# The last 128 output columns: skip product added in the seed of the PSUM bank, plain-copy evacuation, and a store cut into two halves of rows

## The chip, the cores and the metric

The kernel runs on one core of one Trainium2 chip. The metric is the device time of one execution in microseconds (us). The kernel before takes 177.33 us, the median of three runs (177.13, 177.33 and 177.41).

The engines of the core are named as in the profile: PE is TensorE (matrix products), PEld its weight loads, DVE is VectorE, ACT is ScalarE, POOL is GpSimd and SP is SyncE, which does nothing here but issue DMAs. ACT issues a few DMAs too. The engines run their own instruction queues strictly in order and wait for each other through counting semaphores.

## The reference

Two blocks read the same layer-normed rows and their results are added to the input. Block A is a diagonal state-space model, block B a gated feed-forward. The input x has 2048 rows of D = 512 columns, the state P = 512, the hidden width F = 1376; inputs and output are bfloat16.

```python
def _A_ref(x, ...):                      # x is the normed input
    Lam_bar = exp(dt * Lam)
    Bu = einsum("bld,pd->blp", x, B_bar)
    for t in range(L): h = Lam_bar * h + Bu[:, t]; hs.append(h)
    return 2.0 * einsum("blp,dp->bld", hseq, Cmat).real + x * Dskip
def _B_ref(x, w_gate, w_up, w_down):
    return (gelu(x @ w_gate) * (x @ w_up)) @ w_down
xn = layernorm(x)
return x + _A_ref(xn, ...) + _B_ref(xn, ...)
```

So every output element is a sum of four things: x itself, the skip product xn * Dskip, the product of the states with C, and the product of the hidden activations with w_down.

## The kernel before

**Tiling.** The 2048 rows are four blocks of 512 rows; a block is four row tiles of 128 rows (tile number tt = 4 * block + j). Per block the program does: layer norm (LN, LN_act), a transpose of the normed rows by DMA (TR), the two feed-forward products (GU), the input product of the state model (BU), the recurrence on DVE (CHAIN: rotations by cosine and sine tables around a scan), and last the output product (DN). DN(b) adds, for each row tile j, eleven matmuls over the hidden activations (`hidden`) and eight over the states (`states`) into one PSUM bank of 128 x 512 fp32.

**Who adds what in DN.** `seed` (L873 to L876) writes x into the PSUM bank with an ACT copy before the first matmul of the tile; all matmuls accumulate on top of it. XD holds the skip product xn * Dskip (made on DVE, L671). `store` (L897 to L905) evacuates the bank: DVE adds XD to it and writes bfloat16 into one of four OUTB buffers (L902), and a DMA stores the 128 rows (L904).

**The last row tile.** DN(3, tail=384) cuts the fourth tile of the last block into columns 0 to 383 (its own bank) and columns 384 to 511 (an extra bank, `xbank`). Each part has its seed, 19 matmuls, evacuation and store; the store of the 384 columns is issued from ACT, every other one from SP. The 128-column part is the last work of the program.

**The start.** Block 0 is the only one whose feed-forward is computed in part with the rows as stationary operand, from centred but not yet scaled rows: `GT_k` and `GT_mm` (L696 to L714) fill a bank with gate columns beside up columns, for row tile j and column part u (u = 0, 1, 2 are 256 columns wide, u = 3 is 128). `GT_evac` (L716 to L726) empties it: ACT takes the gelu of the gate half (L721), DVE multiplies by the up half and writes H0[j] (L724, called "H0 product" below). The scale 1/sqrt(var) of the layer norm goes in there as a per-row scalar. Eight banks are in use, so the later parts reuse banks of the earlier ones:

```python
for (j, u), bank in zip([(3, 0), (3, 1), (0, 2), (0, 3), (1, 2), (1, 3), (2, 2), (2, 3), (3, 2), (3, 3)],
                        (6, 7, 0, 1, 2, 3, 4, 5, 0, 7)):
    GT_mm(j, u, bank)
    GT_evac(j, u, bank)
```

Part (3, 2) is thus computed into bank 0, which part (0, 2) had six parts earlier; the matmuls of (3, 2) need the gelu and the H0 product of (0, 2) to be done. The six parts before this loop use banks 0 to 5, as acc(j, u) = 2 * j + u for j < 3, u < 2.

**The parameters of the state model.** Three rows of 512 parameters are loaded and transposed by a DMA on the SP queue (`tr_par`, L515, behind the weight loads of `load_W`). `params` (L556 to L565) starts from them: POOL computes exp(log_dt) with one power instruction (L557), DVE multiplies it with Lambda_im (L558, called "theta product" below) and goes on with a few tiny instructions (L559 to L565).

**What sets the order of each queue.** The program is recorded first and then ordered by a planner in the kernel itself (class Sched). Every recorded operation has a duration written out by hand and its dependencies from the buffers it reads and writes. PE and SP keep the order in which they were recorded. DVE, ACT and POOL do not: a list scheduler chooses for them, in time order, the ready operation with the earliest due time. The due times come from a backward pass from the end of the plan; forward and backward passes alternate six times (`schedule`, L136 to L148) and the order with the shortest planned span is taken. `emit` (L286 to L337) then writes the queues, with waits on the counting semaphores where an operation needs another engine's result. A DMA counts in the plan as 2000 ns plus one ns per 350 bytes, behind the DMAs planned before it. The backward pass starts from the last operations of the program, so durations and dependencies there take part in every due time.

**The end.** `emit` also makes SP wait for the stores: before its second-to-last DMA for all stores but the last five, before its last DMA for the next three, and after it for the last two.

Of the kernel before, what the change touches and what calls it, by code (L numbers as in the profile page):

```python
# [9 lines left out]
ALU = mybir.AluOpType  # L10
ACTF = mybir.ActivationFunctionType
# [66 lines left out]
class Sched:  # L78
# [212 lines left out]
    def emit(self):  # L291
        nc, es = self.nc, self.es
        order = self.order
        esem = {}
        for e in ENGINES:
            if any(op.kind == "eng" for op in order[e]):
                esem[e] = es.enter_context(nc.semaphore("q_" + e))
        cnt = {e: 0 for e in ENGINES}
        nd = 0
        for e in ENGINES:  # L300
            for op in order[e]:
                if op.kind == "eng":
                    cnt[e] += 1
                    op.sem, op.val = esem[e], cnt[e]
                else:
                    op.sem, op.val = es.enter_context(nc.semaphore("d%d" % nd)), 16
                    nd += 1
        self.n_sems = len(esem) + nd
        plan = {}
        nwait = 0  # L310
        for e in ENGINES:
            seen = {}
            prog = []
            for op in order[e]:
                need = {}
                for d in op.deps:
                    if d.eng == e and (d is op.behind or d.kind == "eng" and e == "tensor"):
                        continue
                    key = ("e", d.eng) if d.kind == "eng" else ("d", d.id)
                    if seen.get(key, 0) >= d.val:  # L320
                        continue
                    if key not in need or need[key].val < d.val:
                        need[key] = d
                for key, d in need.items():
                    seen[key] = d.val
                waits = [(d.sem, d.val) for d in need.values()]
                nwait += len(waits)
                prog.append((waits, op))
            plan[e] = prog
        self.n_waits = nwait  # L330
        final_waits = [(op.sem, 16) for op in sorted(self.out_ops, key=lambda o: o.finish)]

        for e in ENGINES:
            h = getattr(nc, e)
            for n, (waits, op) in enumerate(plan[e]):
                if e == "sync" and n >= len(plan[e]) - 2:
                    for (s, v) in (final_waits[:-5] if n < len(plan[e]) - 1 else final_waits[-5:-2]):  # L337
                        h.wait_ge(s, v)
                    h.nop(nofuse=True)
                for (s, v) in waits:  # L340
                    h.wait_ge(s, v)
                op.fn(h).then_inc(op.sem, 1 if op.kind == "eng" else 16)
        for (s, v) in final_waits[-2:]:
            nc.sync.wait_ge(s, v)

# [9 lines left out]
def d_pe(n_list):  # L355
    return sum(n / 2.4 + 2.5 for n in n_list)
def d_dve_tt2x(n): return 100.0 + 0.52 * n
def d_dve_1x(n): return 100.0 + 1.04 * n
# [3 lines left out]
def d_act(n, ptr=0): return 190.0 + 0.833 * n + 90.0 * ptr  # L362
# [3 lines left out]
def build(nc, ins, out):  # L366
    with ExitStack() as es:
        E = es.enter_context
        S = Sched(nc, es)
# [3 lines left out]
        PS = [E(nc.psum_tensor("PS%d" % i, [128, 512], F32)) for i in range(8)]  # L373
        BANK = [Buf("bank%d" % i, "ps", i, i + 1) for i in range(8)]

        def ring(parent, name, n):
            return [A.sub(parent, "%s%d" % (name, i), i) for i in range(n)]
# [14 lines left out]
        X = ring(X_all, "X", NT)  # L392
# [72 lines left out]
        V = lambda fn, dur, r, w, tag="", after=(): S.op("vector", fn, dur, r, w, tag, after)  # L465
        ACT = lambda fn, dur, r, w, tag="", after=(): S.op("scalar", fn, dur, r, w, tag, after)
# [81 lines left out]
        def next_bank():  # L548
            b_ = rstate["n"] % 8
            rstate["n"] += 1  # L550
            return b_
# [316 lines left out]
        def DN(b, split=False, tail=None):  # L868
            k2, k3 = b % 2, b % 3
            banks = [next_bank() for _ in range(4)]  # L870
            xbank = next_bank() if tail else None

            def seed(j, c0=0, c1=D):  # L873
                tt, bank = 4 * b + j, banks[j]
                bank = banks[j] if c0 == 0 else xbank
                ACT(lambda e: e.activation(PS[bank][:, c0:c1], X[tt].ap[:, c0:c1], ACTF.Copy), d_act(c1 - c0), [X[tt]], [BANK[bank]], "seed")  # L876

            def mms(j, ops, last, rds, c0, c1):
                bank = banks[j] if c0 == 0 else xbank

                def f(e):
                    ins_ = None
                    for n, (l_, r_) in enumerate(ops):
                        ins_ = e.matmul(PS[bank][:, c0:c1], l_[:, 128 * j:128 * (j + 1)], r_[:, c0:c1], start=False,  # L884
                                        stop=last and n == len(ops) - 1, skip_group_check=True)
                    return ins_
                PE(f, d_pe([c1 - c0] * len(ops)), rds + [BANK[bank]], [BANK[bank]], "DN%d" % b)

            def hidden(j, c0=0, c1=D):
                ops = [(HTt[k2][ft].ap[0:FROWS[ft], :], WD.ap[0:FROWS[ft], ft, :]) for ft in range(KF)]  # L890
                mms(j, ops, False, [HTt[k2][ft] for ft in range(KF)] + WDc, c0, c1)

            def states(j, c0=0, c1=D):
                ops = [(SSc[k3][s][c].ap, CT[c][s].ap) for s in range(KP) for c in range(2)]
                mms(j, ops, True, [SSs[k3][s] for s in range(KP)] + [CT[c][s] for c in range(2) for s in range(KP)], c0, c1)

            def store(j, c0=0, c1=D):  # L897
                tt = 4 * b + j
                bank = banks[j] if c0 == 0 else xbank
                ko = tt % 4  # L900
                ob = OUTB[ko] if c1 - c0 == D else Buf("OUTBp%d" % c0, "sb", OUTB[ko].lo + 2 * c0, OUTB[ko].lo + 2 * c1)
                V(lambda e: e.tensor_tensor(OUTB[ko].ap[:, c0:c1], PS[bank][:, c0:c1], XD[tt].ap[:, c0:c1], ALU.add),  # L902
                  d_dve_1x(c1 - c0), [BANK[bank], XD[tt]], [ob], "evO")
                S.dma(lambda e: e.dma_start(out[0, 128 * tt:128 * (tt + 1), c0:c1], OUTB[ko].ap[:, c0:c1]),  # L904
                      256 * (c1 - c0), reads=[ob], is_output=True, tag="st_out", queue="scalar" if c1 - c0 == tail else "sync")  # L905

            if split:
                for j in range(4):
                    seed(j); hidden(j)
                for j in range(4):  # L910
                    states(j); store(j)
            elif tail:
                for j in range(3):
                    seed(j); hidden(j)
                for j in range(3):
                    states(j); store(j)
                parts = ((0, tail), (tail, D))
                for c in parts:
                    seed(3, *c)
                for c in parts:  # L920
                    hidden(3, *c); states(3, *c); store(3, *c)
            else:
                for j in range(4):
                    seed(j); hidden(j); states(j); store(j)
# [185 lines left out]
```

## Time and profile before

| | us |
|---|---|
| median of three runs (lowest to highest) | 177.33 (177.13 to 177.41) |
| the profiled execution, its own time | 176.71 |
| span of its profile, first to last instruction or packet | 175.4 |
| time around the span in that execution | 1.3 |
| PE busy, share of the span | 172.7, 98% |
| DVE busy, share of the span | 158.5, 90% |
| ACT busy, share of the span | 95.2, 54% |
| POOL busy, share of the span | 9.9, 6% |

The profile is that of one execution. Its page lists the busy time of each engine, the chain of work that ended last, and groups of instructions by source line. Further views give instructions in order of time, the waits, and the granted TensorE clock, which is 1.00 in every stretch of this run. A busy engine on the page is not one that sets the end; whether it does is read from the chain and from what its successor waited for.

### The profile page before, as it was taken

The page shows a single profiled execution, that of the slowest core. Times are in us where ns is not written, and L with a number is a line of the kernel's source. Part 1 is how long each engine was busy: PE and PEld are TensorE (multiplying, and loading weights), DVE is VectorE, ACT ScalarE, POOL GpSimd, SP SyncE. Part 2 cuts the span into 40 slices and gives each one's busy share as a digit, 9 for nine tenths or more (in the row PEclk, how much of TensorE's full clock was granted, in tenths as well). Part 3 has the DMA queues.
Part 4 walks back from the last instruction along what each step waited for, and adds up shares of the span by engine and source line. Part 5 has one row for each costly group of instructions (what it writes and reads, how often), then busy time and mean ns, then how long its engine had stood idle before and what let it go on. Part 6 is the DMA issues. An engine that isn't in the chain of part 4 may idle for free.

```text
span 175.4 us, 2533 instructions
## 1 busy us (share of the span) xinstructions
PE 172.7 (98%) x895; PEld 85.0 (48%) x895; DVE 158.5 (90%) x279; ACT 95.2 (54%) x187; POOL 9.9 (6%) x24
## 2 busy tenths in 40 slices
PE   8999999999999999999999999999999999999995
PEld 2646464845544444444644444444464444444454
DVE  5897999987989999789899999997999999999931
ACT  5476678999766997473676792000667970000000
POOL 4122220220000000002000000000000000000000
DMA  5999999477699400002024000002001000000312
GB/s 142 265 340 191 221 206 154 32 130 142 106 250 344 74 0 2 0 30 89 4 53 98 0 0 0 4 0 90 30 0 34 0 0 0 0 0 0 123 62 62
DMA packets 32421, 14.37 MB, mean 82 GB/s; under 512 B 23736, under 2 KB 32408, under 8 KB 32408
## 3 DMA queue, kind: packets, MB, share of 16 engines
q1 hardware_dynamic: 31952, 13.84, 34.6%
q10 hardware_dynamic: 456, 0.36, 0.6%
q8 instruction: 7, 0.11, 0.3%
q14 instruction: 6, 0.05, 0.1%
HBM read 6.46 MB, written 2.10 MB: 49 GB/s over the span
## 4 chain that ended last, share of the span: by engine, by line
PE 98%; DVE 0%; issue 0%
PE PS L884 37%; PE PS L843 32%; PE PS L749 16%; PE PS L712 4%; PE PS L701 3%; PE PS L817 3%; PE PS L933 2%; PE PS L684 1%; DVE arena L902 0%; PE PS L940 0%
## 5 line engine op out<-in xcount | busy, mean ns | idle before, releaser
L884 PE MATMUL PS<-arena 128*128 128x512 bf16 (+3 forms) x323 | 66.2, 366 | 0.0
L843 PE MATMUL PS<-arena 128*128 128x512 bf16 x264 | 58.1, 379 | 0.0
L884 PEld LDWEIGHTS PS<-arena 128*128 128x128 bf16 (+1 forms) x323 | 30.8, 98 | 35.2
L843 PEld LDWEIGHTS PS<-arena 128*128 128x128 bf16 x264 | 25.7, 98 | 30.3
L787 DVE TENSOR_TENSOR_SCAN arena<-arena 128x512 bf16<-128x512 f32 x32 | 38.8, 1252 | 0.0
L858 ACT ACTIVATE arena<-PS 128x512 bf16<-128x512 f32 x33 | 19.7, 598 | 27.0 <-PE PS L843 24.8
L749 PE MATMUL PS<-arena 128*128 128x512 bf16 (+1 forms) x144 | 28.2, 355 | 0.0
L862 ACT ACTIVATE arena<-PS 128x512 bf16<-128x512 f32 x33 | 19.7, 598 | 5.9 <-PE PS L843 5.8
L749 PEld LDWEIGHTS PS<-arena 128*128 128x128 bf16 x144 | 14.1, 98 | 13.3
L876 ACT ACTIVATE PS<-arena 128x512 f32<-128x512 bf16 (+2 forms) x17 | 9.4, 574 | 18.5 <-DVE arena L902 18.0
L758 ACT ACTIVATE arena<-PS 128x512 bf16<-128x512 f32 x32 | 17.4, 596 | 1.5 <-PE PS L749 1.5
L902 DVE TENSOR_TENSOR arena<-PS,arena 128x512 bf16<-128x512 f32 (+2 forms) x17 | 10.9, 652 | 7.8 <-PE PS L884 7.7
L864 DVE TENSOR_TENSOR arena<-arena 128x512 bf16<-128x512 bf16 x33 | 13.2, 413 | 1.8 <-ACT arena L862 1.6
L776 DVE TENSOR_TENSOR arena<-arena 128x4096 bf16<-128x4096 bf16 (+1 forms) x5 | 9.2, 1858 | 0.8 <-ACT arena L611 0.8
L774 DVE TENSOR_TENSOR arena<-arena 128x4096 bf16<-128x4096 bf16 (+1 forms) x5 | 9.2, 1853 | 0.0
L799 DVE TENSOR_TENSOR arena<-arena 128x4096 bf16<-128x4096 bf16 x4 | 9.1, 2286 | 0.0
L800 DVE TENSOR_TENSOR arena<-arena 128x4096 bf16<-128x4096 bf16 x4 | 9.1, 2284 | 0.0
L615 DVE BATCH_NORM_STATS2 arena<-arena 128x6 f32<-128x512 bf16 x12 | 7.8, 681 | 0.4 <-DMA arena<-in_A_x_dram 0.4
L721 ACT ACTIVATE arena<-PS,arena 128x256 bf16<-128x256 f32 (+1 forms) x16 | 6.3, 447 | 1.9 <-DVE arena L724 1.9
L712 PE MATMUL PS<-arena 128*128 128x512 bf16 (+1 forms) x40 | 7.1, 336 | 0.0
L724 DVE SCALAR_TENSOR_TENSOR arena<-PS,arena 128x256 bf16<-128x256 f32 (+1 forms) x16 | 6.2, 442 | 0.3 <-PE PS L701 0.3
L701 PE MATMUL PS<-arena 128*128 128x256 bf16 (+1 forms) x36 | 6.3, 309 | 0.0
(95 smaller groups left out, 123.4 us busy)
## 6 DMA issues: line engine op xcount, KB each, us to landing
out_dram<-arena SPq DMA_DIRECT2D x15, 128.0 KB, 1.7
arena<-in_A_x_dram SPq DMA_DIRECT2D x3, 512.0 KB, 5.3
arena<-in_B_w_down_dram SPq DMA_DIRECT2D x1, 1280.0 KB, 7.3
arena<-in_B_w_gate_dram SPq DMA_DIRECT2D x4, 128.0 KB, 3.3
arena<-in_B_w_up_dram SPq DMA_DIRECT2D x4, 128.0 KB, 3.2
arena<-in_B_w_gate_dram SPq DMA_DIRECT2D x1, 480.0 KB, 6.5
arena<-in_B_w_up_dram SPq DMA_DIRECT2D x1, 480.0 KB, 7.4
arena<-arena SPq DMA_TRANSPOSE x25, 3.1
```

The lines of the kernel that those rows point to most:

```text
L701: PE(lambda e: e.matmul(dst, XCd(j, k), WGU[:, ws[0]:ws[-1] + 1, k, f0:f1], start=first, stop=k == KD - 1, skip_group_check=True), d_pe([w ...
L712: ins_ = e.matmul(dst, XCd(j, k), WGU[:, :, k, f0:f1], start=(k == 0), stop=(k == KD - 1))
L749: ins_ = e.matmul(PS[bank][:, 128 * j0:128 * j1], BBT[c][dk].ap[:, 128 * s:128 * (s + 1)], XNT[b].ap[:, dk, 128 * j0:128 * j1], start=(dk ...
L758: GATE["evBu"] = ACT(lambda e, bank=bank, k3=k3, s=s, c=c: e.activation(SSc[k3][s][c].ap, PS[bank][:, :], ACTF.Copy), d_act(512), [BANK[ba ...
L787: V(lambda e, g=g, rb=rb, init=init: e.tensor_tensor_scan(g.ap, rb, g.ap, init, ALU.mult, ALU.add), d_dve_scan(512), [g, PA[RRr]] + ([CARc ...
L843: ins_ = e.matmul(PS[bank][0:m, c0:c1], W.ap[:, dk, 128 * ft:128 * ft + m], XNT[b].ap[:, dk, c0:c1], start=(dk == 0), stop=(dk == KD - 1))
L858: GATE["last_gelu"] = ACT(lambda e, bg=bg, kk=kk, m=m: e.activation(GG[kk].ap[0:m, :], PS[bg][0:m, :], ACTF.Gelu_apprx_tanh), d_act(512), ...
L862: ACT(lambda e, bu=bu, kk=kk, m=m: e.activation(UPB[kk].ap[0:m, :], PS[bu][0:m, :], ACTF.Copy), d_act(512), [BANK[bu]], [UPB[kk]], "evU")
L864: V(lambda e, kk=kk, m=m, ft=ft, k2=k2: e.tensor_tensor(HTt[k2][ft].ap[0:m, :], GG[kk].ap[0:m, :], UPB[kk].ap[0:m, :], ALU.mult), d_dve_tt ...
L876: ACT(lambda e: e.activation(PS[bank][:, c0:c1], X[tt].ap[:, c0:c1], ACTF.Copy), d_act(c1 - c0), [X[tt]], [BANK[bank]], "seed")
L884: ins_ = e.matmul(PS[bank][:, c0:c1], l_[:, 128 * j:128 * (j + 1)], r_[:, c0:c1], start=False, stop=last and n == len(ops) - 1, skip_group ...
L902: V(lambda e: e.tensor_tensor(OUTB[ko].ap[:, c0:c1], PS[bank][:, c0:c1], XD[tt].ap[:, c0:c1], ALU.add), d_dve_1x(c1 - c0), [BANK[bank], XD ...
```

## The change

For columns 384 to 511 of the last row tile, and only there:

- The seed is made by DVE instead of ACT: one addition x + XD goes into the PSUM bank.
- The evacuation is a plain DVE copy of the bank into OUTB, since XD is already in the sum.
- The store of 128 rows x 128 columns becomes two DMAs of 64 rows each, one issued from SP and one from ACT.
- There is one store more, so the counts of `emit` move by one: SP waits before its second-to-last DMA for all stores but the last six, before its last DMA for the next three, and then for the last three in two steps.

```diff
@@ emit
-                    for (s, v) in (final_waits[:-5] if n < len(plan[e]) - 1 else final_waits[-5:-2]):
+                    for (s, v) in (final_waits[:-6] if n < len(plan[e]) - 1 else final_waits[-6:-3]):
                         h.wait_ge(s, v)
                     h.nop(nofuse=True)
...
+        nc.sync.wait_ge(*final_waits[-3])
+        nc.sync.nop(nofuse=True)
         for (s, v) in final_waits[-2:]:
             nc.sync.wait_ge(s, v)
@@ seed
-                ACT(lambda e: e.activation(PS[bank][:, c0:c1], X[tt].ap[:, c0:c1], ACTF.Copy), d_act(c1 - c0), [X[tt]], [BANK[bank]], "seed")
+                if c0:
+                    V(lambda e: e.tensor_tensor(PS[bank][:, c0:c1], X[tt].ap[:, c0:c1], XD[tt].ap[:, c0:c1], ALU.add),
+                      d_dve_1x(c1 - c0), [X[tt], XD[tt]], [BANK[bank]], "seed")
+                else:
+                    ACT(lambda e: e.activation(PS[bank][:, c0:c1], X[tt].ap[:, c0:c1], ACTF.Copy), d_act(c1 - c0), [X[tt]], [BANK[bank]], "seed")
@@ store
+                if c0:
+                    V(lambda e: e.tensor_copy(OUTB[ko].ap[:, c0:c1], PS[bank][:, c0:c1]), d_dve_1x(c1 - c0), [BANK[bank]], [ob], "evO")
+                    for n, q in enumerate(("sync", "scalar")):
+                        p0, p1 = 64 * n, 64 * (n + 1)
+                        S.dma(lambda e, p0=p0, p1=p1: e.dma_start(out[0, 128 * tt + p0:128 * tt + p1, c0:c1], OUTB[ko].ap[p0:p1, c0:c1]),
+                              128 * (c1 - c0), reads=[ob], is_output=True, tag="st_out", queue=q)
+                    return
                 V(lambda e: e.tensor_tensor(OUTB[ko].ap[:, c0:c1], PS[bank][:, c0:c1], XD[tt].ap[:, c0:c1], ALU.add),
```

The planner runs again on the changed program, so the queues of DVE, ACT and POOL are ordered anew from the first instruction on; the queues of PE and SP keep their order.

## The prediction

> **What bounds the kernel now.** I read the page's busy times and its chain of waits first.
>
> ```profile
> PE 172.7 (98%) x895; PEld 85.0 (48%) x895; DVE 158.5 (90%) x279; ACT 95.2 (54%) x187; POOL 9.9 (6%) x24
> ...
> PE 98%; DVE 0%; issue 0%
> ```
>
> The chain is PE from end to end, with only the last evacuation and store behind it. A busy PE may still be waiting inside, so I looked at its pace, by windows of 5 us (columns: window, its length, then busy time and instruction count of PE, PEld, DVE, ACT and POOL, granted clock, DMA share, GB/s):
>
> ```profile
> 110.00:115.00 5.00, 5.00 (x25) 2.26 (x24) 5.00 (x8) 0.00 (x0) 0.00 (x0) 1.00 0.00 0
> ```
>
> About 23 new matmuls of 512 columns start in 5 us, one per 0.216 us, and the pace is the same in every such window from 45 us to the end (more, narrower matmuls in a few). So PE never waits there. Two things follow. First, what the change takes from DVE or ACT in the middle is worth nothing, and only what lies behind the last matmul can be won. Second, any new wait of PE, at any place, is added to the end in full, because PE has no slack later to take it back. The planner orders DVE, ACT and POOL anew for the changed program, so I compared those queues, not only the edited lines.
>
> **The edited lines, at the end.** The timeline of the last 3 us (start, length, engine, line, shapes, idle time before):
>
> ```profile
> 172.61 0.56 DVE L902 TENSOR_TENSOR arena<-PS,arena 128x384 bf16<-128x384 f32 x1 [2.40 <-PE PS L884]
> 173.19 0.38 ACTq L904 DMA_DIRECT2D out_dram<-arena  x1
> 173.57 0.29 DVE L902 TENSOR_TENSOR arena<-PS,arena 128x128 bf16<-128x128 f32 x1 [0.41 <-PE PS L884]
> 173.89 0.33 SPq L904 DMA_DIRECT2D out_dram<-arena  x1
> ```
>
> Behind the last matmul (173.55) lie an evacuation of 0.29 us and a store, issued at 173.89, that closes the span at 175.4.
>
> *Evacuation.* L902 takes 0.682, 0.557 and 0.291 us for 512, 384 and 128 columns: (0.682-0.291)/384 = 1.02 ns per column over 0.16 us. No DVE copy out of PSUM is in the trace. At the same pace per column and the same start it is 0.29, a gain of nothing; at half the pace per column 0.16+0.065 = 0.226, a gain of 0.065. A loss I exclude, since it reads one operand less. I take -0.03, the middle. [...]
>
> *Seed.* ACT loses a 0.28 us copy (L876, 161.70) that nobody was near to needing: the bank's matmuls come 10 us later. DVE gains an addition of 128 columns, at most the 0.29 of L902. It sits in the DVE queue between the skip products, after the evacuation that frees the bank. DVE has 0.32 us idle before the evacuation at 166.06 and 1.03, 1.04 and 2.40 us before the next ones. Price zero; without that cover a store in the middle of DN(3) would leave 0.3 us later, also for nothing, as four matmul groups lie behind it.
>
> *Store.* The rows are the landings from issue:
>
> ```profile
> out_dram<-arena SPq DMA_DIRECT2D x15, 128.0 KB, 1.7
> out_dram<-arena ACTq DMA_DIRECT2D x1, 96.0 KB, 1.7
> out_dram<-arena SPq DMA_DIRECT2D x1, 32.0 KB, 1.4
> ```
>
> On SP, 96 KB less is 0.3 us less, so 16 KB less is 0.05 us. ACT's 96 KB landed like SP's 128 KB, so ACT is up to 0.1 us slower, and its issue took 0.378 against 0.332 us. The end is that of the later half: from -0.05 (both as fast as SP's slope says) to +0.15 (ACT's delay, its issue, no gain from size). ACT has issued its 384-column store by 173.57 and is free. I take 0, near the 32 KB row. [...] SP's waits ahead of its last two DMAs cover the same three stores, long landed; the 384-column store lands at about 174.9, before the end.
>
> Sum of the edited lines: -0.03 us, bounds -0.12 to +0.15.
>
> **The queues that are ordered anew.** The difference begins near 10 us, at the H0 products (L724), and there is one place where PE's cover is small. Before:
>
> ```profile
> 10.98 1.66 DVE L724 SCALAR_TENSOR_TENSOR arena<-PS,arena 128x256 bf16<-128x256 f32 x4 [0.34 <-PE PS L701]
> 12.55 0.40 DVE L634 TENSOR_SCALAR arena<-arena 128x512 bf16<-128x512 bf16 x1
> 12.88 2.04 DVE L724 SCALAR_TENSOR_TENSOR arena<-PS,arena 128x256 bf16<-128x256 f32 x5
> 16.08 0.16 DVE L558 TENSOR_TENSOR arena<-arena 128x4 f32<-128x4 bf16 x1 [1.16 <-POOL arena L557]
> 16.27 0.17 DVE L561 TENSOR_SCALAR arena<-arena 128x4 f32<-128x4 f32 x1
> ...
> 14.95 1.02 POOL L557 TENSOR_TENSOR arena<-arena 128x4 bf16<-128x4 f32 x1 [4.87 <-DMA arena<-arena]
> ```
>
> DVE does nine H0 products, then waits 1.16 us for the theta product (L558), whose input POOL finishes at 15.97 after waiting for the parameter transpose, issued at 7.8 and 7.1 us on its way. In the changed program the theta product stands after six H0 products instead of nine. The three moved behind it are those of parts (3,1), (0,2) and (3,0), in this order. DVE is strictly in order, so these three now wait for the transpose.
>
> *When the theta product can run.* SP's order, the weight loads ahead of the transpose, and the POOL queue from the power instructions on are unchanged (POOL only swaps start-up fills), so it again runs at 16.08. DVE reaches it at about 13.3: in the old row of five, 12.88 to 14.92, the second ends at 13.74, and L634, 0.4 us, no longer stands ahead of it but in the idle time before the second product. DVE idles some 2.8 us instead of 1.16.
>
> *When part (0,2) is freed.* The row of five gives (2.04-0.47)/4 = 0.39 us from one product to the next and 0.47 for one alone. The first moved product starts 0.08 to 0.20 after the theta product starts (0.08 is the distance from L561 to the next, independent, product at 16.35; 0.19 the distance from L558 to L561, which needs its result). The second starts 0.39 later and ends 0.47 after that: 16.08+0.08+0.39+0.47 = 17.02, or 17.14.
>
> *When PE wants it.* Part (3,2) goes into bank 0, which part (0,2) filled.
>
> ```profile
> 10.79 7.09 PE L712 MATMUL PS<-arena 128*128 128x512 bf16 x40
> 17.71 2.54 PE L843 MATMUL PS<-arena 128*128 128x512 bf16 x11
> ```
>
> The 40 matmuls of L712 fill 10.79 to 17.71: 24 of 512 and 16 of 256 columns, so 6.92/64 = 0.108 us per 256 columns. Ahead of (3,2) are 20 wide and 12 narrow ones, 52 units or 5.62 us, so it starts at 16.41. Before, the product of (0,2) was done at 14.92, 1.5 us of cover. Now it ends at 17.02 to 17.14, and 0.06 us later (the shortest distance that I find from an ACT or DVE result to the waiting matmul, in the first 10 us) PE goes on: 17.08 to 17.20, a new wait of **0.67 to 0.79 us**. I take 0.70.
>
> *Is it given back, or followed by more?* PE has no slack afterwards, so it stays. The next parts need the gelu and product of (1,2), (1,3) and (2,2); stepping through the two queues with the same rows (0.47 and 0.39 for a gelu or product, 0.35 for a narrow one, 0.48 for L602, three gelu buffers in rotation), the products end about 0.5, 0.3 and 0.7 us before PE wants their banks. That cover of 0.3 us is the thinnest. Later the same stepping leaves over 1.3 us everywhere. One other move: a gelu (0.47) now stands ahead of the transposed copy L689 at 9.91. It can begin when its bank is complete, about 9.68, and lets go of ACT 0.36 later, so L689 ends at 10.63 instead of 10.51, still before PE needs it at 10.79. Price zero; without that cover 0.1 us.
>
> **Sum.** On the profiled execution: 176.71 + 0.70 - 0.03 = 177.38, span 176.1. The three runs have a median 0.62 above that execution, so as a median 177.33 + 0.67 = **178.0 us**.
>
> **The rivals.**
>
> *1. No new wait (chance 0.14).* For it: it takes only 0.7 us, and a parameter transpose that lands at 14.2 instead of 14.9 would remove it. Against it: the transpose is issued behind two 480 KB weight loads, which were 6.5 and 7.4 us on their way, and nothing ahead of it changes. Then only the end counts: 177.33-0.03 = 177.3, within 177.2 to 177.5.
>
> *2. A gain at the end (0.04 beyond 0.2%).* Even with no new wait the best sum is -0.12 us, 177.2, which is 0.07%; a gain that shows would need PE to start earlier, and PE's waits in the first 9 us are for loads that stay where they are.
>
> *3. More than one wait (0.10, part of the slower cases).* DVE is late by 1.3 us from 17 us on. If the cover of 0.3 us at part (1,3)'s bank goes, PE waits again, 0.1 to 0.5 us: 178.1 to 178.5. A wait of 0.7 us could also cost PE its pace: the seven start-up matmuls (L933, 3.14 us) ran at about half of it, and 3 us at half pace would lose 1.5 us, 179.5. The one idle stretch of PE in the trace of about 0.2 us, near 9 us, was followed by full pace. [...]
>
> **How the numbers follow.** Likeliest case 0.72: the wait as worked out, 178.0, its own range 177.9 to 178.3 (177.33 and 0.67-0.12 to 0.79+0.15). Rival 1 is 0.14, rival 2 0.04, rival 3 0.10. The range of 8 in 10 takes part of rival 3 and little of rival 1: 177.5 to 178.4. What a measurement can tell from no change is about 0.2%, 0.35 us here. The likeliest case is 0.38% slower, so slower 0.82, same 0.14, faster 0.04.
>
> **What would show it.** In the changed profile: the theta product preceded by some 2.8 us of DVE idle time put down to POOL, with three H0 products of 256 columns behind it; the second matmul row of PE with a gap of about 0.7 us before part (3,2), so the first L843 group at 18.4 instead of 17.71; everything after it shifted by that and nothing more; a copy of about 0.26 us as the last DVE row and two store issues landing within 1.5 us. Wrong: PE's L712 group still 6.9 us long (rival 1), or a shift that grows again before 25 us (rival 3).

## The result, and the profile after

The changed kernel takes 178.07 us (median of 15 runs, 177.69 to 178.38), the kernel before beside it 177.13 (15 runs, 176.71 to 177.94). The ratio is 1.0046, 95% interval 1.0032 to 1.0061: slower by 0.94 us between the medians. The forecast was 178.0 us, slower. The profiled execution took 177.69 us with a span of 176.4, against 176.71 and 175.4, so it shows 1.0 us to account for.

The page of the changed kernel, its engines and its chain of waits:

```profile
PE 171.9 (97%) x880; PEld 84.7 (48%) x895; DVE 159.8 (91%) x280; ACT 94.9 (54%) x186; POOL 12.9 (7%) x24
...
PE 89%; DMA 4%; SPq 4%; issue 1%; POOL 1%; DVE 1%; DVEq 0%; POOLq 0%
```

The chain was PE throughout; it now starts with SP's issues of the early loads and passes the DMA of the parameter transpose, POOL and DVE before it gets to PE. (PE shows 880 matmuls for 895 weight loads: 15 records are missing, one of them at 18.1 us below.) The same chain in order of time, around the place where it enters PE (start, length, what):

```profile
7.70 6.73 DMA arena<-arena
...
14.57 1.03 POOL arena L559
...
15.70 0.06 DVE arena L560
...
16.20 0.49 DVE arena L726
16.69 0.14 issue
16.82 1.46 PE PS L714 x8
```

These are the steps of the prediction: parameter transpose, power on POOL (L557 before, L559 now), theta product (L560), the H0 product of part (0,2), and PE's matmuls of part (3,2). The DVE and PE timelines give the lengths:

```profile
11.44 2.04 DVE L726 SCALAR_TENSOR_TENSOR arena<-PS,arena 128x256 bf16<-128x256 f32 x5
15.70 0.16 DVE L560 TENSOR_TENSOR arena<-arena 128x4 f32<-128x4 bf16 x1 [2.21 <-POOL arena L559]
15.80 1.27 DVE L726 SCALAR_TENSOR_TENSOR arena<-PS,arena 128x256 bf16<-128x256 f32 x3
```

```profile
10.73 5.79 PE L714 MATMUL PS<-arena 128*128 128x512 bf16 x32
16.82 1.46 PE L714 MATMUL PS<-arena 128*128 128x512 bf16 x8 [0.30 <-DVE arena L726]
18.34 2.97 PE L845 MATMUL PS<-arena 128*128 128x512 bf16 x13
```

DVE is idle for 2.21 us ahead of the theta product and has the three products behind it. PE's 40 matmuls, one group before, are cut in two; 32 of them take 5.62 us at the pace of before, so part (3,2) starts 16.82 - 10.73 - 5.62 = 0.47 us late. (The row's bracket says 0.30: it counts from the end of a matmul of 0.38 us, while in an unbroken stretch the next one starts 0.216 us after the start of the one before. Waits of PE are taken from start to start here.) PE's stream began 0.06 us earlier than in the execution of before, so its end is 0.41 us later. The end of the changed kernel:

```profile
173.34 0.56 DVE L915 TENSOR_TENSOR arena<-PS,arena 128x384 bf16<-128x384 f32 x1 [2.72 <-PE PS L890]
173.93 0.38 ACTq L917 DMA_DIRECT2D out_dram<-arena  x1
173.98 0.29 DVE L909 CAST arena<-PS 128x128 bf16<-128x128 f32 x1
174.30 0.56 SPq L912 DMA_DIRECT2D out_dram<-arena  x1
174.35 0.55 ACTq L912 DMA_DIRECT2D out_dram<-arena  x1
```

And its stores of the last columns, from the list of DMA issues (size, time from issue to landing):

```profile
out_dram<-arena SPq DMA_DIRECT2D x1, 16.0 KB, 1.8
out_dram<-arena ACTq DMA_DIRECT2D x1, 16.0 KB, 2.0
```

From the start of the last evacuation to the end of the span it was 175.4 - 173.57 = 1.8 us before and is 176.4 - 173.98 = 2.4 now. So the 1.0 us is 0.41 us of PE and 0.6 us behind it. The second part was not forecast: half the bytes take longer to issue (0.56 and 0.55 against 0.33 us) and longer to land (1.8 and 2.0 against 1.4).

### The profile page after: what moved, and what is told of

Same layout as the page of the kernel before. It is cut to its first block, busy times and chain, and to the rows that moved or that the text cites. A ratio compares the mean times of both kernels' runs of the same rounds, so it can differ in the third digit from the quotient of the medians.

```text
span 176.4 us, 2514 instructions
## 1 busy us (share of the span) xinstructions
PE 171.9 (97%) x880; PEld 84.7 (48%) x895; DVE 159.8 (91%) x280; ACT 94.9 (54%) x186; POOL 12.9 (7%) x24
## 4 chain that ended last, share of the span: by engine, by line
PE 89%; DMA 4%; SPq 4%; issue 1%; POOL 1%; DVE 1%; DVEq 0%; POOLq 0%
PE PS L890 37%; PE PS L845 32%; PE PS L751 16%; DMA arena<-arena 4%; PE PS L819 3%; SPq L490 2%; SPq L495 1%; PE PS L714 1%; POOL arena L559 1%; SPq L499 0%; DVE arena L726 0%; DVE arena L909 0%; DVE arena L560 0%; SPq L341 0%; DVEq L341 0%
## 5 line engine op out<-in xcount | busy, mean ns | idle before, releaser
L845 PE MATMUL PS<-arena 128*128 128x512 bf16 x257 | 57.1, 379 | 0.4
L915 DVE TENSOR_TENSOR arena<-PS,arena 128x512 bf16<-128x512 f32 (+1 forms) x16 | 10.6, 674 | 6.0 <-PE PS L890 6.0
L882 ACT ACTIVATE PS<-arena 128x512 f32<-128x512 bf16 (+1 forms) x16 | 9.3, 600 | 0.7
L714 PE MATMUL PS<-arena 128*128 128x512 bf16 (+1 forms) x40 | 7.2, 336 | 0.3 <-DVE arena L726 0.3
```

What stands on the lines that cost most here:

```text
L845: ins_ = e.matmul(PS[bank][0:m, c0:c1], W.ap[:, dk, 128 * ft:128 * ft + m], XNT[b].ap[:, dk, c0:c1], start=(dk == 0), stop=(dk == KD - 1))
```

## The experiments

The theory after this reading: two independent losses, an early PE wait behind the moved theta product and a later end because of the split store. The rivals: all of it is the early wait (A), or all of it is the end, the early wait being given back (B). In the first four kernels the planner plans the kernel before; its queues are then edited by hand, so nothing moves that isn't named. Each kernel is compared with runs of the kernel before in the same series, whose medians were 177.06 (first series), 177.25 (second) and 177.05 (third).

**The theta product alone**

```diff
         S.schedule()
+        v = S.order["vector"]
+        th = [o for o in v if o.tag == "th"][0]
+        prods = ...          # H0 products (3, 1), (0, 2), (3, 0)
...
+        v[at:at] = [th] + prods
```

> The kernel before, with one thing changed: in the DVE queue the theta product stands ahead of the H0 products of (3,1), (0,2), (3,0), in this order, as in the changed kernel. The end is as before. Theory (an early PE wait at bank 0 plus a later last landing, together 0.9 us): PE waits 0.4 to 0.8 us ahead of part (3,2) and the time is the kernel before plus 0.4 to 0.8 us. Rival A (the wait is the whole loss): plus 0.9. Rival B (the loss is all at the end, the early wait is given back): within 0.15 of the kernel before.

Measured: 178.36 us, ratio 1.0074 (1.0060 to 1.0089), 1.3 us more than before. That is above what either theory gave. Its PE timeline:

```profile
11.09 5.79 PE L712 MATMUL PS<-arena 128*128 128x512 bf16 x32
17.40 1.46 PE L712 MATMUL PS<-arena 128*128 128x512 bf16 x8 [0.52 <-DVE arena L724]
19.40 0.81 PE L843 MATMUL PS<-arena 128*128 128x512 bf16 x3 [0.55 <-ACT arena L721]
```

The first wait is there: 17.40 - 11.09 - 5.62 = 0.69 us. A second one follows: the last eight L712 matmuls take 1.30 us, so the next product should start at 18.70 and starts at 19.40. The row puts that down to ACT. What PE waits for, by the order of the banks in the program, is the bank of part (1,2), whose H0 product ends on DVE at 18.20 + 0.85 = 19.05, late because its gelu was late. In this kernel ACT still has the narrow gelu of (0,3) (128 columns) ahead of the wide one of (1,2), and the narrow one needs the gelu buffer that the last of the three moved products frees at 16.38 + 1.27 = 17.65. ACT stands idle until then:

```profile
17.73 1.77 ACT L721 ACTIVATE arena<-PS,arena 128x128 bf16<-128x128 f32 x5 [3.13 <-DVE arena L561]
```

The changed kernel has the two the other way round, and does the wide one as soon as the first moved product is done:

```profile
16.37 0.47 ACT L723 ACTIVATE arena<-PS,arena 128x256 bf16<-128x256 f32 x1 [1.93 <-DVE arena L726]
```

The two waits, 1.39 us, account for the time. So moving one tiny instruction is enough for the early wait, nothing is given back later (B falls), and the changed kernel's other moves spared it a second wait of this kind.

**The edits of the end, in parts**

```diff
         S.schedule()
+        S.order["scalar"].remove(op); op.eng, op.fn = "vector", fn      # seed on DVE, behind XD[15]
+        v.insert(v.index(skip) + 1, op)
+        ...                                                             # evacuation: tensor_copy
+        st.fn = fn0                                                     # store: rows 0-63 on SP
+        S.order["scalar"].append(st2)                                   # rows 64-127 on ACT
```

All three edits:

> All three edits of the end, but every DVE, ACT and POOL queue in the order of the kernel before up to the end. Theory: no PE gap near 16 us, the last landing 0.3 to 0.6 us later after the last matmul, time plus 0.3 to 0.6 us. Rival A: within 0.15 of the kernel before. Rival B: plus 0.9.

Measured: 177.76 us, ratio 1.0040 (1.0026 to 1.0054), plus 0.70, a little above what the theory gave; PE's early group runs through in one piece.

Only the split store:

> Only the store of the last 128 columns is cut into two halves of rows (SP and ACT); seed, evacuation and all orders as before. Theory: the whole loss of the end is here, plus 0.3 to 0.6 us, with two issues of some 0.55 us each against one of 0.33. Rival (the copy or the seed on DVE delays the end): within 0.1 of the kernel before.

Measured: 177.71 us, ratio 1.0036 (1.0022 to 1.0049), plus 0.65, a little above the expectation. Its last two issues:

```profile
174.27 0.56 SPq L911 DMA_DIRECT2D out_dram<-arena  x1
174.28 0.56 ACTq L911 DMA_DIRECT2D out_dram<-arena  x1
```

Only seed and copy:

> Only seed on DVE and plain-copy evacuation, one store from SP, orders as before. Theory: within 0.1 us of the kernel before, since the changed kernel's copy took 0.292 us against 0.291. Rival (the copy or the seed on DVE delays the end): plus 0.3 to 0.6 us, with the evacuation of the 384 columns starting late, as it did in the changed kernel (0.4 us after its last wait was met).

Measured: 176.97 us, ratio 0.9994 (0.9979 to 1.0009). The end's loss is the split store alone, and A falls too.

**The changed kernel with one loss taken away**

The theta product put back behind the three products (the same edit as in the first kernel, the other way):

> The changed kernel with the theta product put back behind the three H0 products of (3,1), (0,2), (3,0) in the DVE queue; all else, the split store too, as in the changed kernel. Theory (early wait of 0.3 to 0.5 us plus a later end of 0.6 us): PE's L714 group runs through in 6.9 us, the time is the kernel before plus 0.6. Rival (the other moves in the queues cost as well): plus 0.75 or more, with a gap elsewhere in PE.

Measured: 177.78 us, ratio 1.0035 (1.0019 to 1.0051), plus 0.53; PE's L714 group is one piece again, 10.97 to 17.90.

One store of 128 rows from SP, queues as in the changed kernel:

```diff
         S.schedule()
+        GATE["half0"].fn = GATE["whole"]
+        S.order["scalar"].remove(GATE["half1"])
```

> The changed kernel with its queues as they are, but the last 128 columns stored by one DMA of 128 rows from SP. Theory: the end is as in the kernel before (2.06 us from the start of the last matmul to the end of the span), the early wait at bank 0 stays, the time is the kernel before plus 0.3 to 0.5 us. Rival (the two losses are not independent): plus 0.6 or more.

Measured: 177.53 us, ratio 1.0018 (1.0006 to 1.0031), plus 0.28, just below what the theory gave. In its profiled execution the early wait is 17.22 - 10.84 - 5.62 = 0.76 us:

```profile
10.84 5.79 PE L712 MATMUL PS<-arena 128*128 128x512 bf16 x32
17.22 1.46 PE L712 MATMUL PS<-arena 128*128 128x512 bf16 x8 [0.59 <-DVE arena L724]
```

The two losses, 0.35% and 0.18%, add to 0.53%, within the interval of the whole change (0.32% to 0.61%).

**Why the early wait costs 0.3 us and not 0.7**

PE's L712 group and the theta product start at their own times, the one behind PE's earlier products, the other behind the transpose and POOL, and these move from execution to execution. From the timelines of the eleven profiled executions with the old order of SP's early queue:

| | L712 group starts | theta product starts | distance | PE waits before (3,2) |
|---|---|---|---|---|
| kernel before | 10.79 | 16.08 | 5.29 | - |
| changed kernel | 10.73 | 15.70 | 4.97 | 0.47 |
| theta early | 11.09 | 16.27 | 5.18 | 0.69 |
| changed, one store | 10.84 | 16.09 | 5.25 | 0.76 |
| changed, theta back | 10.97 | 16.24 | 5.27 | - |
| all edits of the end | 11.43 | 16.22 | 4.79 | - |
| split store | 11.16 | 15.54 | 4.38 | - |
| seed and copy | 11.29 | 16.24 | 4.95 | - |
| halves from SP (below) | 11.58 | 16.16 | 4.58 | - |
| one half (below) | 11.46 | 15.90 | 4.44 | - |
| column halves (below) | 10.95 | 15.99 | 5.04 | - |

Where the theta product stands early, the wait is the distance less 4.49 to 4.50 us, in all three executions. The distance runs from 4.38 to 5.29, so the wait would run from nothing to 0.80. The execution that the prediction was worked out from has the largest distance of the eleven.

That is no accident, for its 176.71 us is also the shortest time of the kernel before in its series (176.71 to 177.94). In the three profiled executions with neither a wait of PE at this place nor a changed store, the time less the start of PE's group is the same: 176.71 - 10.79 = 165.92 (kernel before), 177.23 - 11.29 = 165.94 (seed and copy) and 177.13 - 11.19 = 165.94 (kernel before with an early transpose, below). So what makes such an execution longer is a later start of PE's group, and then the distance, and with it the wait, is smaller. The runs fit this: the shortest run of the changed kernel with one store is 0.50 us above the shortest of the kernel before (177.20 and 176.70), the longest only 0.05 us above the longest (177.83 and 177.78).

**Taking the lateness away and leaving the order**

```diff
+        q = S.order["sync"]                  # tr_par ahead of the last two weight loads
+        q.remove(tr)
+        q.insert([n for n, o in enumerate(q) if o.tag == "ld_w"][-2], tr)
```

> The changed kernel with one store of the last 128 columns (as in b4_after_one_store), and the parameter transpose issued on SP ahead of the last two weight loads instead of behind them; the queues of DVE, ACT and POOL as in the changed kernel, the theta product still ahead of the three H0 products. Theory (the late transpose makes the wait, not the order in itself): POOL's L557 starts before 12 us, no PE gap before part (3,2), the time equals that of c5_before_transpose_early within 0.15 us. Rival (the order itself costs): still 0.3 us more than c5_before_transpose_early.

> The control of c4_transpose_early: the kernel before with the parameter transpose ahead of the last two weight loads, nothing else. PE did not wait for it in the kernel before, so the time is that of the kernel before within 0.2 us, unless the two weight loads, now later by the transpose's 2 us of issue, come too late for PE near 18 us.

Measured: 177.08 us, ratio 1.0009 (0.9994 to 1.0024), and for the control 177.11 us, ratio 1.0003 (0.9991 to 1.0015). POOL's power instruction starts at 12.43 and 11.91 us, a little later than hoped for in the first. In the first, the theta product in the timeline of DVE, and the timeline of PE:

```profile
13.78 0.15 DVE L558 TENSOR_TENSOR arena<-arena 128x4 f32<-128x4 bf16 x1
```

```profile
11.03 7.09 PE L712 MATMUL PS<-arena 128*128 128x512 bf16 x40
18.48 1.89 PE L843 MATMUL PS<-arena 128*128 128x512 bf16 x8 [0.36 <-DMA arena<-arena]
```

The theta product is still ahead of the three H0 products, but it waits for nothing and PE's group is whole. The late transpose makes the wait; the order only puts the products behind it. In this execution PE's next product is late instead, for another DMA transpose: a whole group takes 17.71 - 10.79 = 6.92 us from start to start, and 18.48 - 11.03 - 6.92 = 0.53 us remain. The control has no such wait (18.11 - 11.19 = 6.92). Its cause was not tried, and the runs show no cost of it on average: the medians of the two kernels differ by 0.03 us. Both intervals reach some 0.2 to 0.3 us to each side, so the times alone would hardly rule out the rival's 0.3 us; that the wait ahead of part (3,2) is gone is read from the timeline.

**What is dear in the split store**

Two halves of rows, both from SP:

> The kernel before with the last store cut into two halves of rows, both issued from SP, one after the other. If issuing from two engines at once is what slows both issues (0.56 against 0.33 us): two issues of 0.33, the last landing 0.3 to 0.4 us later than before. If a DMA of 64 rows costs 0.56 to issue by itself: two of 0.56 in a row, the last landing 0.9 us later.

Measured: 178.78 us, ratio 1.0092 (1.0071 to 1.0114), plus 1.5 us, more than either account gave: the second issue began only 1.02 us after the first, although nothing in the program stood between them.

```profile
174.68 0.56 SPq L911 DMA_DIRECT2D out_dram<-arena  x1
175.70 0.47 SPq L911 DMA_DIRECT2D out_dram<-arena  x1
```

One half alone:

> The kernel before with the last store cut to rows 0 to 63 of the last tile's last 128 columns, issued from SP; rows 64 to 127 of these columns are left out. If two issues at once are the cause: issue 0.33 us, landing 1.4 us or a little less, time within 0.1 of the kernel before. If the 64-row DMA costs more by itself: issue 0.56, landing 1.78, time plus 0.35.

Measured: 177.39 us, ratio 1.0019 (1.0005 to 1.0032), plus 0.14 between the medians and 0.34 by the ratio; the last issue in the timeline, and its row in the list of DMA issues:

```profile
174.57 0.56 SPq L909 DMA_DIRECT2D out_dram<-arena  x1
```

```profile
out_dram<-arena SPq DMA_DIRECT2D x1, 16.0 KB, 1.8
```

The issue of 0.56 and the landing of 1.8 us are there with one half and one queue, so two issues at once are not the cause.

Two halves of columns, 128 rows x 64 columns each, from SP and ACT:

> The kernel before with the last store cut into two halves of columns, 128 rows x 64 columns each, one from SP and one from ACT. If it is the 64 rows that make a DMA dear (0.56 us to issue, landing 1.78): issues of 0.33 and 0.38, landings of 1.4 to 1.7, the end at most 0.3 us later. If any store in two costs the same: the end 0.6 us later, as with the halves of rows.

Measured: 177.47 us, ratio 1.0016 (1.0000 to 1.0033). Its last two issues and their landings:

```profile
174.05 0.33 SPq L911 DMA_DIRECT2D out_dram<-arena  x1
174.06 0.37 ACTq L911 DMA_DIRECT2D out_dram<-arena  x1
```

```profile
out_dram<-arena SPq DMA_DIRECT2D x1, 16.0 KB, 1.4
out_dram<-arena ACTq DMA_DIRECT2D x1, 16.0 KB, 1.6
```

The same 16 KB per DMA, from the same two queues at the same moment, but with 128 rows: the old issue times return, and landings of 1.4 and 1.6 us. So the price has two parts. One is that of a DMA of 64 rows: about 0.35 us more from issue to landing (1.8 us with one half alone against 1.4 in the kernel before; unrounded, the traces of the changed kernel and the kernel before give 1.78 for SP's half and 1.44), 0.23 of them in the issue. The other is that the half from ACT lands last, 0.2 us after SP's with the column halves and 0.2 to 0.4 us with the halves of rows. No run stores so little from ACT alone, so whether ACT's queue is slower by itself or the two stores hinder each other is open. Why 64 rows were dearer to issue than 128 (0.56 against 0.33 us) is open too; no run here looks into it.

## Why the prediction was right

The sign was right, and one of its two causes was forecast. That the sum was right to 0.07 us, 178.0 against 178.07, is luck. The early wait was put at 0.70 and cost 0.28 us (-0.42); the edited lines were put at -0.03 and the split store alone cost 0.65 (+0.68); and the kernel before, put at 177.33, had a median of 177.13 beside the changed one (-0.20). About two thirds of the loss come from a term that the prediction put at 0.

*Where the path lies.* Right: what the change took from ACT and gave to DVE did not count (177.06 before, 176.97 with seed and copy), and the early PE wait was not given back. From the start of PE's next product to the last evacuation it is 155.86 us in the kernel before (17.71 to 173.57) and in the changed kernel with one store (18.52 to 174.38).

*The early wait.* Its place, its releaser and its chain were as forecast, and the step "the first moved product 0.08 to 0.20 after the theta product" too (15.70 to 15.80). So was the length of the chain: PE followed the theta product after 16.82 - 15.70 = 1.12 us, the upper end of the 1.00 to 1.12 forecast. The size was not: 0.70 forecast, 0.47 in the profiled execution, plus 0.28 between the medians with one store. The step that failed is "it again runs at 16.08", together with 16.41 for PE: both times were taken from one execution, and their distance varies by 0.9 us from one to the next. The step to the median failed with it. The prediction added the wait of an execution of 176.71 us to a median of 177.33; by the account above such a median execution starts PE's group at 177.33 - 165.93 = 11.40, and with the theta product at 16.08 the wait is an estimated 16.08 - 11.40 - 4.49 = 0.19 us.

*The store.* This is the step that was wrong: "I take 0", with bounds of -0.05 to +0.15; measured plus 0.65 alone. The stores it was drawn from move 128 rows each, and the slope was taken by bytes. The larger part is the 64-row DMA's own issue and landing, about 0.35 us with one half alone; the two halves landed 1.8 and 2.0 us after their issue, not within 1.5. The rest is the later landing of ACT's half (0.2 to 0.4 us behind SP's with the halves of rows), whose cause no run shows.

*The copy and the seed.* The copy takes 0.29 us, as the addition did: the upper of the two bounds; no run shows the -0.03. The pace of the case's own rows, 1.02 ns per column over 0.16 us, is met (0.16 + 0.13 = 0.29). The seed cost nothing that shows (copy and seed together: ratio 0.9994).

*The rivals.* No new wait: it would have been so in an execution like that of the split store, whose distance of 4.38 leaves nothing. So the rival hangs on the transpose's landing, as the prediction said, but on PE's own start as much. More than one wait: not in the changed kernel. When the theta product was moved without the other moves a second one did appear, but at the bank of (1,2) and of 0.70 us, where the prediction had named (1,3) and 0.1 to 0.5 us. PE's pace did not fall: with one store, after the wait of 0.76 us, the eight matmuls (12 units of 256 columns) took 18.52 - 17.22 = 1.30 us, the 0.108 us per unit of the kernel before, and the granted clock of that run is 1.00. No longer wait of PE than 0.76 us is in the table above, so what a longer one would cost is not shown.

## What to carry to other kernels

Where a planner orders the queues, an edit of the last operations is an edit of all of them: compare the queues, look for instructions that wait for a DMA and moved ahead of work that another engine needs, and price what stands behind them. A cover worked out from one profiled execution is one draw; where two streams set it that don't wait for each other, take its spread from several executions. An execution may be short for the very reason that makes its wait long, so its wait can't simply be added to a median: the one of 176.71 us here has the largest distance of the eleven, 5.29 us. Price a DMA by rows of its own shape, not by its bytes: half a store was slower here than the whole, 1.8 against 1.4 us from issue to landing.

## What the runs showed of the hardware that was not expected

- From SP, a store of 64 rows x 256 bytes at the end of this kernel took 0.56 us to issue and 1.8 us to land; 128 rows x 256 bytes took 0.33 and 1.4, and so did 128 rows x 128 bytes.
- Two such 64-row stores in a row from SP cost 1.5 us over the single 128-row store, with 1.02 us between the starts of their issues (0.56 and 0.47 us long).
- In the changed kernel DVE began the evacuation of the 384 columns at 173.34 us, 0.64 us before the last one, where the kernel before has 0.96 between them. Both kernels that take one loss away but keep the changed queues show 0.64 or 0.65 again. It costs nothing here: the last evacuation itself is no later behind PE's work (155.86 us, above). Its cause was not tried.
